# GpSimd's early transfers go ahead of its constants; the scan's first piece goes first; the last tile's outputs share one buffer

## The chip, the cores and the metric

The kernel runs on one core of a Trainium2 chip. Its engines work side by side, each through its own queue of instructions in a fixed order: TensorE (PE; PEld are its weight loads), VectorE (DVE), ScalarE (ACT), GpSimd (POOL) and SyncE (SP, which only issues transfers). Transfers (DMAs) are issued here by GpSimd, SyncE and ScalarE. The metric is the time of one execution on the device in microseconds (us), lower is better.

## What is computed

Causal attention with a selective bias, followed by a layer norm and a two-layer MLP with a residual. There are 8 batches of 8 heads, 576 positions and a head size of 64; the model width is 512 and the hidden width 2048.

```python
# attention, for each batch and head
cum    = np.cumsum(np.maximum(s, 0.0), axis=-1)
scores = q @ k.T / sqrt(64) + np.minimum(-(cum[:, None] - cum[None, :]), 0.0)
attn   = softmax(where(causal, -1e9, scores))
x      = attn @ v                      # heads side by side: (8, 576, 512)
# MLP, for each position
xn  = (x - mean) / sqrt(var + 1e-6) * g_ln
out = x + np.maximum(xn @ w_ch1, 0.0) @ w_ch2
```

## The kernel before, in words

**Scores with the bias inside.** The cumulated sum of s is added to the scores by the matmul itself: k and q get four more rows behind their 64 (68 in all), which hold cum split into three bf16 pieces (hi, mid, lo) and the constants 1 and -1. The tiles `kq[0..2]` hold k and q transposed, with 4 heads each (a group; there are 16). Positions are cut into four tiles of 128 and one of 64.

**Batch 0 is treated apart.** Its k and q come as rows into `rowb`: tile 0 by way of two f32 tiles that SyncE (k) and ScalarE (q) load and ScalarE casts (steps `ck` and `cq`), tiles 1 to 4 by GpSimd transfers that cast on the way (line 148). The bias pieces are added to the rows as columns, and TensorE transposes both (step T), from PSUM to `kq[0]` and `kq[1]` (step e, the evacuation). Groups 2 to 5 come as pairs of heads (line 152, tiles kp and qp, pairs 4 to 11), are transposed by TensorE (step Q, line 276), and get their four extra rows by small SyncE transfers of the pieces (`aug`, lines 212 and 214). The later groups come as rows by SyncE and are transposed by the DMA engines.

**The start.** s is loaded to `c_in`. Three cuts of it (positions 0 to 127, 128 to 255, 256 to 575) go each through relu, scan (the running sum), hi, sub, mid, lo; then TensorE transposes the pieces (step tc) and VectorE puts them into `rowb` (step bc). The steps W are idle matmuls that keep TensorE running.

**Order.** Nothing is scheduled by a tool: the order in which the code issues instructions is the order in every queue. First come the constants and the first transfers; then PLAN, a list of words written out by hand, each a step with its tile, group and engine (`e.0.1:D` is the evacuation of tile 0, group 1 on VectorE); then a loop over the remaining heads n, from head 18 on. The waits between engines come from the tiles that an instruction reads and writes.

**GpSimd's queue.** All transfers that cast come from GpSimd, in one order: the k, q and v tiles of batch 0, the first quarter ("part 0") of the first weight w1, pair 4, tile 4 of batch 0, then w1 part 1, pair 5, w1 part 2, the five v tiles of batch 1, pair 6, w1 part 3, and the second weight and pairs 7 and 8. Between them stand memsets of constants: the pads and constant rows of `kq[2]`, the column of ones in `v_bf[1]` (65th column of each head, which makes the attention's sums), the pad of `er` (the exponentials), constants of `cT`.

**MLP.** `units` of four matmuls each, in a queue of their own that PLAN (words u and U) and the loop draw on, fill TensorE between the attention steps: `mlp1` (line 539) against w1 with a relu to `hT`, `mlp2` (line 557) against the second weight. At its end `mlp2` adds the residual into a buffer `yo` (line 566) and sends it out. The pool `yop` has three such buffers, taken in turn. The last 64 positions of all batches are put together, two batches a tile, and come last (`mixed_units`); the last of these four tiles is cut into three pieces of columns (256, 128, 128), each with a `yo` of its own, and each tile goes out in two transfers, from SyncE and ScalarE (lines 591 and 592).

Of the kernel before, what the change touches and what calls it, by code (L numbers as in the profile page):

```python
# [9 lines left out]
F32 = mybir.dt.float32  # L10
BF16 = mybir.dt.bfloat16
AX = mybir.AxisListType
ALU = mybir.AluOpType
ACT = mybir.ActivationFunctionType

P = 128
# [3 lines left out]
def kernel(  # L20
# [11 lines left out]
    nc = tc.nc  # L32
    B, H, S, D = q.shape
    Dm, Dh = moe_w_ch1.shape
# [4 lines left out]
    NF = S // P  # L39
    NT = NF + 1  # L40
    TL = S - NF * P
    SP = NT * P
    BH = B * H
    KA = D + 4
    OB, OC, OD = 512, 1024, 1536
    EW = 1664
# [5 lines left out]
    KT = 96  # L52
# [10 lines left out]
    yop = ctx.enter_context(tc.tile_pool(name="yop", bufs=3))  # L63
# [8 lines left out]
    ident = const.tile([P, P], BF16, name="ident")  # L72
    maskT = const.tile([P, P], BF16, name="maskT")
# [3 lines left out]
    gb = const.tile([P, Dm], F32, name="gb")  # L77
    rstd = const.tile([P, B, NT], F32, name="rstd")
    mhalf = const.tile([P, 8], F32, name="mhalf")
# [3 lines left out]
    v_bf = [const.tile([P, NT, H, D + 1], BF16, name=f"v_bf{i}") for i in range(2)]  # L83


    kq = [const.tile([P, 2, G, SP], BF16, name=f"kq{i}") for i in range(3)]
# [7 lines left out]
    er = const.tile([P, 4, EW], BF16, name="er")  # L94
# [7 lines left out]
    rowb = const.tile([P, NT, 2 * H, KA], BF16, name="rowb")  # L102
# [26 lines left out]
    def tile_src(kind, t):  # L129
        pn = P if t < NF else TL  # L130
        src = k if kind == "k" else q
        return src[0, :, t * P : t * P + pn, :].rearrange("h s d -> s h d")
# [6 lines left out]
    def ld_tile(kind, t, eng):  # L139
        tmp = stage.tile([P, H, D], F32, name="tiletmp", tag="st")  # L140
        eng.dma_start(out=tmp, in_=tile_src(kind, t))
        loaded[kind, t] = tmp
# [4 lines left out]
    def ld_cast_tile(kind, t):  # L147
        nc.gpsimd.dma_start(out=tile_dst(kind, t), in_=tile_src(kind, t))  # L148

    def ld_cast(kind, g):  # L150
        ready[kind, g] = pair_tile(kind)
        nc.gpsimd.dma_start(out=ready[kind, g][0:QP], in_=pair_src(kind, g))

    def ld_cast_pair(g):
        ld_cast("k", g)
        ld_cast("q", g)

    def ld_cast_v(b, t):
        pn = P if t < NF else TL
        nc.gpsimd.dma_start(  # L160
            out=v_bf[b % 2][:pn, t, :, 0:D],
            in_=v[b, :, t * P : t * P + pn, :].rearrange("h s d -> s h d"),
        )
# [34 lines left out]
    def ld_w1(c):  # L198
        sl = slice(c * 512, (c + 1) * 512)
        nc.gpsimd.dma_start(out=w1_bf[:, :, sl], in_=w1_r[:, :, sl])  # L200
# [348 lines left out]
            nc.scalar.activation(out=hT[:, fb, :], in_=ph, func=ACT.Relu)  # L549

    py = {}

    def mlp2(t, quarter, x, rs, dst, c0=0, c1=512):
        if quarter == 0:
            py[t] = ps_m.tile([P, Dm], F32, name="py", tag="m")[:, 0 : c1 - c0]
        for fb in range(quarter * 4, quarter * 4 + 4):
            nc.tensor.matmul(  # L557
                py[t],
                lhsT=hT[:, fb, t * P : (t + 1) * P],
                rhs=w2_bf[:, fb, c0:c1],  # L560
                start=(fb == 0),
                stop=(fb == FB - 1),
            )
        if quarter == 3:
            yo = yop.tile([P, Dm], F32, name="yo", tag="yo")[:, 0 : c1 - c0]
            nc.vector.scalar_tensor_tensor(  # L566
                out=yo, in0=py[t], scalar=rs, in1=x[:, c0:c1], op0=ALU.mult, op1=ALU.add
            )
            dst(yo, c0, c1)


    def chunk_units(xT_of, of_t, last=False):
        units = [lambda fb=fb: mlp1(xT_of(), fb) for fb in range(FB)]
        for t in range(NF):
            halves = ((0, 256), (256, 384), (384, 512)) if last and t == NF - 1 else ((0, 512),)
            for c in halves:
                for qr in range(4):
                    units.append(lambda t=t, qr=qr, c=c: mlp2(t, qr, *of_t(t), *c))
        return units
# [27 lines left out]
    def keep_warm(n):  # L607
        w = ps_t.tile([P, 512], F32, name="idle", tag="tr")
        for _ in range(n):
            nc.tensor.matmul(w, lhsT=zeros[:, 0:P], rhs=zeros, start=True, stop=True)  # L610
# [7 lines left out]
    )  # L618
    nc.sync.dma_start(out=c_in, in_=s.rearrange("b h s -> (b h) s"))
    ld_tile("k", 0, nc.sync)  # L620

    nc.vector.memset(zeros.bitcast(F32), 0.0)
    nc.vector.memset(warm, 0.0)
# [5 lines left out]
    nc.vector.memset(rowb[:, :, H : 2 * H, D + 1 : KA], 1.0)  # L629
    nc.vector.memset(v_bf[0][:, 0:NF, :, D : D + 1], 1.0)  # L630
    nc.vector.memset(v_bf[0][0:TL, NF, :, D : D + 1], 1.0)
    for i in range(2):
        nc.vector.memset(kq[i][0:KA, 0, :, S:SP], 0.0)
    nc.vector.memset(eight, 1.0 / scale)
    nc.vector.memset(mhalf, -0.5)
    nc.vector.memset(c3[BH:KT], 0.0)
    nc.vector.memset(rowb[TL:KT, NF], 0.0)
    make_identity(nc, ident)
    nc.gpsimd.memset(maskT, 0.0)
    nc.gpsimd.affine_select(  # L640
        out=maskT,
        in_=maskT,
        compare_op=ALU.is_ge,
        fill=-1.0e30,
        base=0,
        pattern=[[1, P]],
        channel_multiplier=-1,
    )
    for t in range(1, NF):
        ld_cast_tile("k", t)  # L650
        ld_cast_tile("q", t)
        ld_cast_v(0, t - 1)
        if t == 1:
            nc.gpsimd.dma_start(out=gb, in_=moe_g_ln.partition_broadcast(P))
    ld_cast_v(0, NF - 1)
    ld_w1(0)
    ld_cast_pair(4)
    ld_cast_tile("k", NF)
    ld_cast_tile("q", NF)
    ld_cast_v(0, NF)  # L660

    nc.gpsimd.memset(kq[2][:, :, :, S:SP], 0.0)
    for u, two in ((0, -1.0058441162109375), (1, 1.0019378662109375)):
        nc.gpsimd.memset(kq[2][D:P, u].bitcast(F32)[:, :, 0 : S // 2], two)  # L664
    ld_w1(1)
    nc.gpsimd.memset(v_bf[1][:, 0:NF, :, D : D + 1], 1.0)
    nc.gpsimd.memset(v_bf[1][0:TL, NF, :, D : D + 1], 1.0)
    for i in range(2):
        nc.gpsimd.memset(v_bf[i][TL:P, NF, :, :], 0.0)
    nc.gpsimd.memset(er[:, :, OD:EW], 0.0)  # L670
    ld_cast_pair(5)
    ld_w1(2)
    nc.gpsimd.memset(cT[:, :, 0, :, 0], -1.0)
    nc.gpsimd.memset(cT[:, :, 1, :, 1:4], 1.0)
    for t in range(NT):
        ld_cast_v(1, t)
    ld_cast_pair(6)
    ld_w1(3)
    ld_w2(0)
    ld_cast_pair(7)  # L680
# [200 lines left out]
    def pv_next():  # L881
# [5 lines left out]
        if ph_ == 7:  # L887
# [6 lines left out]
            out=c_in[:, 0:P], in0=c_in[:, 0:P], scalar=0.0, in1=eight, op0=ALU.max, op1=ALU.mult  # L894
# [18 lines left out]
        "M": piece,  # L913
        "r": piece_relu,
        "W": lambda n: keep_warm(n),
        "Sk": last_scores,
        "xk": last_exp,
        "relur": lambda: nc.scalar.activation(
            out=c_in[:, P:S], in_=c_in[:, P:S], func=ACT.Relu, scale=1.0 / scale
# [20 lines left out]
    }  # L940

    PLAN = """
        relu.0 scan.0 relur hi.0 scan.1 sub.0 hi.1 ck sub.1 mid.0 W.4 mid.1 lo.0 tc.0 bc.0 W.2
        cq T.0.0 scan.2 lo.1 hi.2 e.0.0:D T.0.1 W.2 e.0.1:D sub.2 tc.1 S.0.0.0 x.0.0.0 S.0.1.0
        bc.1 V.0.0 T.1.1 mid.2 N.0.0 x.0.1.0 T.1.0 V.0.1 e.1.1:D S.1.1.0 lo.2 e.1.0:A tc.2 bc.2
        x.1.1.0 S.1.0.0 T.2.0 S.1.1.1 bc.4 T.2.1 e.2.0:D x.1.0.0 S.1.0.1 x.1.1.1 S.2.0.0 T.3.0
        V.1.1 N.0.1 e.2.1:D aug x.2.0.0 x.1.0.1 L.0 S.2.1.0 S.2.0.1 x.2.1.0 S.2.1.1 V.1.0
        e.3.0:D x.2.0.1 T.3.1 N.1.0 N.1.1 S.2.1.2 x.2.1.1 S.2.0.2 x.2.1.2 x.2.0.2 L.1 S.3.0.0
# [112 lines left out]
```

## Time and profile before

| | us |
|---|---|
| median of 3 runs | 353.77 (353.52 to 355.91) |
| the profiled execution | 354.29 |
| its span | 352.6 |
| TensorE busy | 344.4 |
| VectorE busy | 192.2 |
| ScalarE busy | 190.4 |
| GpSimd busy | 162.0 |

The span goes from the first to the last instruction of the program; the execution's own time has 1.7 us around it. In a line of the timeline stand the start in us, the duration, the engine, the line of code, the operation, what is written and read, the shape and the number of instructions taken together, and, in brackets, how long the engine had been idle and what ended that. In the chain of waits stand start, duration and what the chain ran through. A transfer's landing is counted from the start of its issue. GpSimd's rows of transfers are the issuing alone; the data follow later.

In the first 45 us the DMA engines are busy nearly throughout; TensorE has its useful work from 7.65 us on (the first transposes of batch 0) and from 12.2 us on it runs almost without a gap.

### The profile page before, as it was taken

Reading aid. Unit: us, or ns where it says so; the run is one execution under the profiler, and the core shown is the slowest. Engines: PE = TensorE matmul, PEld = TensorE weight load, DVE = VectorE, ACT = ScalarE, POOL = GpSimd, SP = SyncE. Lnnn points to the kernel's source line nnn. Section 1 sums busy time; section 2 is a strip of 40 time slices with the busy share of each in tenths; the row PEclk is TensorE's granted clock in tenths of the full one; section 3 lists DMA queues with packets and bytes.
Section 4 is the critical chain, followed back from the end, with each engine's and each line's share of the span. In section 5 each row is a group of like instructions: output and inputs, shape, how many; then the busy total and the mean of one; then the engine's idle time right before and its main releaser. Section 6 shows DMA issues by size and latency. Waiting matters only on the chain.

```text
span 352.6 us, 8239 instructions
## 1 busy us (share of the span) xinstructions
PE 344.4 (98%) x3110; PEld 196.1 (56%) x3110; DVE 192.2 (55%) x519; ACT 190.4 (54%) x365; POOL 162.0 (46%) x334
## 2 busy tenths in 40 slices
PE   7999999999999999999999999999999999999995
PEld 3898666655555555555555555555555544444444
DVE  7788688964366537562655458443844582113112
ACT  4799798977635673367526662576347403402500
POOL 9996587284455736383756365445521010000000
PEclk9999999999999999999999999999999999999999
DMA  9999999899998999999999999999830033011012
GB/s 150 170 164 150 201 204 129 144 176 143 187 188 132 196 210 178 210 198 176 188 199 205 198 180 171 203 160 200 148 108 0 3 81 112 2 59 59 3 41 79
DMA packets 169160, 50.31 MB, mean 143 GB/s; under 512 B 156896, under 2 KB 164512, under 8 KB 169120
## 3 DMA queue, kind: packets, MB, share of 16 engines
q1 hardware_dynamic: 115168, 36.54, 56.0%
q0 software_dynamic: 52432, 12.46, 41.1%
q10 hardware_dynamic: 1520, 0.79, 0.9%
q8 instruction: 24, 0.39, 0.5%
q14 instruction: 16, 0.13, 0.1%
HBM read 37.11 MB, written 9.44 MB: 132 GB/s over the span
## 4 chain that ended last, share of the span: by engine, by line
PE 81%; DMA 7%; POOL 6%; DVE 2%; issue 1%; SPq 1%; POOLq 0%; DVEq 0%
PE ph L539 32%; PE py L557 32%; PE pot L404 7%; DMA w_bf<-in_moe_w_ch_dram 5%; PE sc L326 3%; PE sb L326 3%; PE sa L326 3%; POOL rowb L148 2%; DMA rowtmp<-in_q_dram 2%; POOL v_bf L160 1%; PE trqk L276 1%; DMA out_dram<-yo 1%; DVE yo L566 1%; SPq L170 1%; POOL kq L664 1%
## 5 line engine op out<-in xcount | busy, mean ns | idle before, releaser
L557 PE MATMUL py<-w_bf,hT 128*128 128x512 bf16 (+2 forms) x608 | 133.6, 368 | 0.0
L539 PE MATMUL ph<-xT,w_bf 128*128 128x512 bf16 x480 | 112.5, 379 | 0.7 <-DMA w_bf<-in_moe_w_ch_dram 0.7
L549 ACT ACTIVATE hT<-ph 128x512 bf16<-128x512 f32 x102 | 60.8, 598 | 73.2 <-PE ph L539 73.2
L557 PEld LDWEIGHTS <-hT 128*128 128x128 bf16 x608 | 54.3, 98 | 52.7
L539 PEld LDWEIGHTS <-w_bf 128*128 128x128 bf16 x544 | 49.5, 98 | 51.3 <-issue 0.8
L337 ACT ACTIVATE er<-sa 128x512 bf16<-128x512 f32 x56 | 33.4, 597 | 59.4 <-PE sa L326 53.0
L346 POOL TENSOR_SCALAR_AFFINE_SELECT er<-er 128x256 bf16<-128x256 bf16 x108 | 44.3, 430 | 35.5 <-ACT er L337 34.7
L547 DVE TENSOR_SCALAR hT<-ph 128x512 bf16<-128x512 f32 x34 | 23.5, 692 | 58.0 <-PE ph L539 50.0
L566 DVE SCALAR_TENSOR_TENSOR yo<-py,rstd,xb 128x512 f32<-128x512 f32 x32 | 23.9, 748 | 35.8 <-PE py L557 34.5
L404 PEld LDWEIGHTS <-er 128*128 128x128 bf16 x840 | 32.9, 98 | 13.1 <-POOL er L346 0.9
L326 PEld LDWEIGHTS <-kq 68*128 68x128 bf16 x400 | 28.5, 97 | 19.8
L160 POOL DMA_DIRECT2D v_bf<-in_v_dram x40 | 34.6, 872 | 2.5 <-PE pot L404 1.8
L404 PE MATMUL pot<-v_bf,er 128*128 128x65 bf16 x840 | 34.9, 194 | 0.4 <-POOL er L346 0.4
L337 ACT ACTIVATE er<-sc 128x512 bf16<-128x512 f32 x56 | 34.1, 610 | 0.0
L337 ACT ACTIVATE er<-sb 128x512 bf16<-128x512 f32 x56 | 33.5, 597 | 0.0
L178 POOL CAST rowb<-rowtmp 128x512 bf16<-128x512 f32 (+1 forms) x25 | 15.3, 610 | 34.4 <-DMA rowtmp<-in_k_dram 14.9
L416 DVE RECIPROCAL rinv<-pot 128x5 f32<-128x5 f32 x56 | 10.8, 192 | 36.9 <-PE pot L404 36.8
L178 POOL CAST kq<-rowtmp 128x512 bf16<-128x512 f32 (+1 forms) x25 | 15.4, 616 | 30.9 <-DMA rowtmp<-in_q_dram 27.5
L418 DVE TENSOR_TENSOR xb<-pot,rinv 128x256 f32<-128x256 f32 x56 | 23.8, 425 | 1.9
L494 DVE SCALAR_TENSOR_TENSOR xn<-xb,mv,gb 128x512 bf16<-128x512 f32 x28 | 22.9, 818 | 1.0
L448 DVE BATCH_NORM_STATS2 stats<-xb 128x6 f32<-128x128 f32 (+1 forms) x84 | 21.9, 320 | 0.3
L326 PE MATMUL sc<-kq 68*128 68x256 bf16 (+1 forms) x192 | 21.7, 228 | 0.0
(118 smaller groups left out, 354.4 us busy)
## 6 DMA issues: line engine op xcount, KB each, us to landing
out_dram<-yo SPq DMA_DIRECT2D x32, 256.0 KB
rowtmp<-in_k_dram SPq DMA_DIRECT2D x40, 128.0 KB
rowtmp<-in_q_dram SPq DMA_DIRECT2D x40, 128.0 KB
v_bf<-in_v_dram POOLq DMA_DIRECT2D x32, 128.0 KB, 5.6
w_bf<-in_moe_w_ch_dram POOLq DMA_DIRECT2D x8, 512.0 KB, 9.7
kp<-in_k_dram POOLq DMA_DIRECT2D x8, 144.0 KB, 7.9
qp<-in_q_dram POOLq DMA_DIRECT2D x8, 144.0 KB, 7.9
rowtmp<-in_k_dram SPq DMA_DIRECT2D x10, 64.0 KB
```

The source lines that it names most:

```text
L160: nc.gpsimd.dma_start(out=v_bf[b % 2][:pn, t, :, 0:D], in_=v[b, :, t * P : t * P + pn, :].rearrange("h s d -> s h d"),)
L178: nc.gpsimd.tensor_copy(out=rows[gam % 2][0:pn, t, :, :, 0:D], in_=loaded.pop(("rows", gam, t))[0:pn])
L326: nc.tensor.matmul(a[:, c + a0 - q0 : c + a1 - q0], lhsT=k_cols(b, h, kb), rhs=cols, start=True, stop=not (pe_mask and diag),)
L337: nc.scalar.activation(out=e[:, o : o + 512], in_=a, func=ACT.Exp, scale=scale)
L346: nc.gpsimd.affine_select(out=two, in_=two, compare_op=ALU.is_ge, fill=0.0, base=0, pattern=[[0, 2], [1, P]], channel_multiplier=-1,)
L404: nc.tensor.matmul(pot[:, t, :], lhsT=e[:, o : o + P], rhs=vv[:, kb, h, :], start=(kb == 0), stop=(kb == last),)
L418: nc.vector.tensor_tensor(out=xb[b][:, :, hs], in0=pot[:, 0:NF, 0:D], in1=rinv[:, 0:NF].unsqueeze(2).to_broadcast([P, NF, D]), op=ALU.mult,)
L539: nc.tensor.matmul(ph, lhsT=w1_bf[:, kd, fb * P : (fb + 1) * P], rhs=xT[:, :, kd, :], start=(kd == 0), stop=(kd == KD - 1),)
L547: nc.vector.tensor_scalar_max(out=hT[:, fb, :], in0=ph, scalar1=0.0)
L549: nc.scalar.activation(out=hT[:, fb, :], in_=ph, func=ACT.Relu)
L557: nc.tensor.matmul(py[t], lhsT=hT[:, fb, t * P : (t + 1) * P], rhs=w2_bf[:, fb, c0:c1], start=(fb == 0), stop=(fb == FB - 1),)
L566: nc.vector.scalar_tensor_tensor(out=yo, in0=py[t], scalar=rs, in1=x[:, c0:c1], op0=ALU.mult, op1=ALU.add)
```

## The change

GpSimd's queue: `ident` and `maskT` are made after the first and second group of three loads, no longer ahead of all. The load of `gb` (the gain of the norm) goes to SyncE. w1 part 1 goes ahead of the memsets of `kq[2]`, and pair 5 ahead of its constant rows. The pads of `kq[0]` and `kq[1]` come to GpSimd from VectorE. The five v tiles of batch 1 go ahead of the pad of `er` and of the ones of `v_bf[1]`, pair 6 ahead of the constants of `cT`.

VectorE's queue: two memsets (`mhalf`, and rows 64 to 95 of the last row tile) go from the start into PLAN, as the step m. In PLAN the first cut's mid and lo go ahead of the second cut's sub, and `cq` goes from behind `bc` to right behind `relur`.

Output: the three pieces of the last tile (and each whole tile) take columns of one `yo`.

```diff
+    yos = {}
...
         if quarter == 3:
-            yo = yop.tile([P, Dm], F32, name="yo", tag="yo")[:, 0 : c1 - c0]
+            if c0 == 0:
+                yos[t] = yop.tile([P, Dm], F32, name="yo", tag="yo")
+            yo = yos[t][:, c0:c1]
...
     ld_tile("k", 0, nc.sync)
+    nc.sync.dma_start(out=gb, in_=moe_g_ln.partition_broadcast(P))
...
-    for i in range(2):
-        nc.vector.memset(kq[i][0:KA, 0, :, S:SP], 0.0)
     nc.vector.memset(eight, 1.0 / scale)
-    nc.vector.memset(mhalf, -0.5)
     nc.vector.memset(c3[BH:KT], 0.0)
-    nc.vector.memset(rowb[TL:KT, NF], 0.0)
-    make_identity(nc, ident)
-    nc.gpsimd.memset(maskT, 0.0)
-    nc.gpsimd.affine_select(
...
     for t in range(1, NF):
         ld_cast_tile("k", t)
         ld_cast_tile("q", t)
         ld_cast_v(0, t - 1)
         if t == 1:
-            nc.gpsimd.dma_start(out=gb, in_=moe_g_ln.partition_broadcast(P))
+            make_identity(nc, ident)
+        if t == 2:
+            nc.gpsimd.memset(maskT, 0.0)
+            nc.gpsimd.affine_select(
...
     ld_cast_v(0, NF - 1)
     ld_w1(0)
     ld_cast_pair(4)
     ld_cast_tile("k", NF)
     ld_cast_tile("q", NF)
     ld_cast_v(0, NF)
-
+    ld_w1(1)
+    for i in range(2):
+        nc.gpsimd.memset(kq[i][0:KA, 0, :, S:SP], 0.0)
     nc.gpsimd.memset(kq[2][:, :, :, S:SP], 0.0)
+    ld_cast_pair(5)
     for u, two in ((0, -1.0058441162109375), (1, 1.0019378662109375)):
         nc.gpsimd.memset(kq[2][D:P, u].bitcast(F32)[:, :, 0 : S // 2], two)
-    ld_w1(1)
+    ld_w1(2)
+    for i in range(2):
+        nc.gpsimd.memset(v_bf[i][TL:P, NF, :, :], 0.0)
+    for t in range(NT):
+        ld_cast_v(1, t)
+    nc.gpsimd.memset(er[:, :, OD:EW], 0.0)
     nc.gpsimd.memset(v_bf[1][:, 0:NF, :, D : D + 1], 1.0)
     nc.gpsimd.memset(v_bf[1][0:TL, NF, :, D : D + 1], 1.0)
-    for i in range(2):
-        nc.gpsimd.memset(v_bf[i][TL:P, NF, :, :], 0.0)
-    nc.gpsimd.memset(er[:, :, OD:EW], 0.0)
-    ld_cast_pair(5)
-    ld_w1(2)
+    ld_cast_pair(6)
     nc.gpsimd.memset(cT[:, :, 0, :, 0], -1.0)
     nc.gpsimd.memset(cT[:, :, 1, :, 1:4], 1.0)
-    for t in range(NT):
-        ld_cast_v(1, t)
-    ld_cast_pair(6)
     ld_w1(3)
     ld_w2(0)
     ld_cast_pair(7)
...
+        "m": lambda: (nc.vector.memset(rowb[TL:KT, NF], 0.0), nc.vector.memset(mhalf, -0.5)),
...
-        relu.0 scan.0 relur hi.0 scan.1 sub.0 hi.1 ck sub.1 mid.0 W.4 mid.1 lo.0 tc.0 bc.0 W.2
-        cq T.0.0 scan.2 lo.1 hi.2 e.0.0:D T.0.1 W.2 e.0.1:D sub.2 tc.1 S.0.0.0 x.0.0.0 S.0.1.0
-        bc.1 V.0.0 T.1.1 mid.2 N.0.0 x.0.1.0 T.1.0 V.0.1 e.1.1:D S.1.1.0 lo.2 e.1.0:A tc.2 bc.2
+        relu.0 scan.0 relur cq hi.0 scan.1 sub.0 hi.1 ck mid.0 lo.0 W.4 sub.1 mid.1 tc.0 bc.0 W.2
+        T.0.0 scan.2 lo.1 hi.2 e.0.0:D T.0.1 W.2 e.0.1:D sub.2 tc.1 S.0.0.0 x.0.0.0 S.0.1.0
+        bc.1 V.0.0 T.1.1 mid.2 N.0.0 x.0.1.0 T.1.0 V.0.1 e.1.1:D S.1.1.0 lo.2 m e.1.0:A tc.2 bc.2
```

More of the change, by code (lines that the diff above doesn't have):

```diff
@@ L631 @@
     nc.vector.memset(v_bf[0][0:TL, NF, :, D : D + 1], 1.0)
-    for i in range(2):
-        nc.vector.memset(kq[i][0:KA, 0, :, S:SP], 0.0)
     nc.vector.memset(eight, 1.0 / scale)
-    nc.vector.memset(mhalf, -0.5)
     nc.vector.memset(c3[BH:KT], 0.0)
-    nc.vector.memset(rowb[TL:KT, NF], 0.0)
-    make_identity(nc, ident)
-    nc.gpsimd.memset(maskT, 0.0)
-    nc.gpsimd.affine_select(
[L641 to L648, printed above, removed]
     for t in range(1, NF):
@@ L653 @@
         if t == 1:
-            nc.gpsimd.dma_start(out=gb, in_=moe_g_ln.partition_broadcast(P))
+            make_identity(nc, ident)
+        if t == 2:
+            nc.gpsimd.memset(maskT, 0.0)
+            nc.gpsimd.affine_select(
+                out=maskT,
+                in_=maskT,
+                compare_op=ALU.is_ge,
+                fill=-1.0e30,
+                base=0,
+                pattern=[[1, P]],
+                channel_multiplier=-1,
+            )
     ld_cast_v(0, NF - 1)
```

## The prediction

> **What bounds the kernel now.** I read the page first, then the chain of waits, the timelines of GpSimd and TensorE for the first 60 us, single transfers' times to landing, and last the timeline of the tail.
>
> ```profile
> PE 344.4 (98%) x3110; PEld 196.1 (56%) x3110; DVE 192.2 (55%) x519; ACT 190.4 (54%) x365; POOL 162.0 (46%) x334
> PE ph L539 <- DMA w_bf<-in_moe_w_ch_dram: 0.7, 1, 0.7
> ```
>
> TensorE is busy for 344.4 of 352.6 us and has one long wait after the start, 0.7 us. Its order is fixed by the plan, so a change can gain only at the two ends and in such waits. It can lose wherever an operand lands after its matmul's turn. The execution took 354.29 us, 1.7 over its span; the runs' median is 353.77, 0.52 less. I sum against 354.29 and take 0.52 off at the end.
>
> The timeline of VectorE at the start, then of GpSimd:
>
> ```profile
> 3.84 0.51 DVE L637 MEMSET rowb<- 32x544 uint32 x1
> 4.38 0.28 DVE L893 SCALAR_TENSOR_TENSOR c_in<-c_in,eight 64x128 f32<-64x128 f32 x1
> ...
> 4.65 0.60 POOL L654 DMA_DIRECT2D gb<-in_moe_g_ln_dram  x1
> 15.31 0.69 POOL L662 MEMSET kq<- 128x512 bf16 x1
> 16.06 2.05 POOL L664 MEMSET kq<- 64x1152 f32 x2
> 18.07 0.77 POOL L200 DMA_DIRECT2D w_bf<-in_moe_w_ch_dram  x1
> 18.88 0.25 POOL L666 MEMSET v_bf<- 128x32 bf16 x1
> 24.32 4.23 POOL L160 DMA_DIRECT2D v_bf<-in_v_dram  x5
> ...
> 31.05 0.79 POOL L200 DMA_DIRECT2D w_bf<-in_moe_w_ch_dram  x1 [1.23 <-DMA w_bf<-in_moe_w_ch_dram]
> 35.47 0.64 POOL L152 DMA_DIRECT2D qp<-in_q_dram  x1 [1.08 <-DMA v_bf<-in_v_dram]
> ```
>
> Two things are to be seen. The s work begins when VectorE's last memset ends, though ACT had c_in at 3.87. And GpSimd waits: w1's part 3 (31.05) for w1's part 2, q of pair 7 (35.47) for the third v tile of batch 1. Both were issued eight transfers earlier: at most eight of GpSimd's are in flight.
>
> **Head.** VectorE loses from its queue two kq memsets (0.31), mhalf (0.07) and rowb (0.51). So relu.0 starts when c_in is there, 3.87 instead of 4.38: 0.5 earlier. mid.0 and lo.0 (0.28 each) no longer stand behind sub.1 (0.28, which waited 0.18 for hi.1 on ACT): 0.4 more. ident, made after three loads, is ready near 4.1 and first needed near 5; maskT near 7.3, needed near 8.4. The two moved memsets of step m (0.58) fit the 0.70 that VectorE idles ahead of 13.19. cq (0.61) moves into the 1.42 that ACT idles ahead of hi.1 (5.86); its tile's packets end at 4.3 in the trace's DMA records, so it costs nothing, and up to 0.3 should the tile come later. What is late next is the k tile: ck now starts at 6.28, right after hi.1, and the T.0.0 transposes follow it. GpSimd's first load starts at 0.81 instead of 1.84, so its packets run beside the k tile's. Bounds: -0.86 (k tile unharmed) to +0.2 (k tile 0.9 late). I take -0.4, the middle, since no row separates them.
>
> In the windows, 42 to 44 us has a DMA share of 1.25 at 200 GB/s, 32 to 34 us 2.90 at 126: more packets at once do not mean more bytes. [...]
>
> **GpSimd's early transfers.** Without the four constants ahead (0.81 to 1.84) the first three loads go 1.03 earlier. gb's issue (0.56) leaves for SyncE, where nothing is queued behind it before 18.14. From the third pair of loads on, everything is 0.56 earlier up to v's last tile, whose issue ends near 14.75. w1 part 1 follows at once (18.07 before), then the two kq pads taken from VectorE (bounds 0.3, VectorE's own time, to 1.5, twice the step of 0.75 of the 128x512 memset; I take 0.75, since together they have fewer elements), kq2's pad 0.75, and k of pair 5 near 17.1. q of pair 5 must wait: with gb gone from the order, the transfer eight before it is w1 part 0, landed at 11.28 + 7.9 = 19.1, now near 18.6. So the two constant fills (2.0) end near 21.2 and w1 part 2 goes at 21.2 (21.98 before). TensorE used all of these with time to spare, so the earlier landings are worth nothing by themselves. The other moved fills are covered too: er's pad (now near 27) is first written over at 34.97, v_bf's tail rows (near 22) are read from 33.5.
>
> The SyncE transfers of c (line 212, 18.14) wait for those fills: they start 3.1 later, near 21.2. Their last packets end at 23.6 in the trace's DMA records, so near 26.7. Scores s.8 read them at 27.99, with the head's gain 27.6. Bounds 0 to 1.3 of wait; I take 0, as the row leaves 0.9. Such a wait would be swallowed by the next one.
>
> **The step that decides.** The ones columns of v_bf[1] (line 666, 0.33 with 667) are now filled after the five loads of that tile, on the queue that issued them. In the trace's records the first v load (3.79) carries a wait on VectorE, whose only earlier work on that tile is its ones columns; the two rowb loads in front carry none. So columns and load of this tile, though disjoint, are ordered against each other. Turned round, the memset waits until the loads have *landed*, and GpSimd's queue stands behind it: pair 6, two cT memsets, w1 part 3, w2 part 0, pairs 7 and 8, w2 part 1, the masks. Call the landing of batch 1's last v tile T. Before:
>
> ```profile
> L160 POOL DMA_DIRECT2D v_bf<-in_v_dram x1: 747/747/747, 27.8 to 27.8; - x1
> DMA to landing us min/median/max: 9.4/9.4/9.4
> ...
> L152 POOL DMA_DIRECT2D qp<-in_q_dram x1: 636/636/636, 35.5 to 35.5; - x1
> DMA to landing us min/median/max: 8.9/8.9/8.9
> ...
> L160 POOL DMA_DIRECT2D v_bf<-in_v_dram x1: 896/896/896, 58.8 to 58.8; - x1
> DMA to landing us min/median/max: 3.7/3.7/3.7
> ```
>
> That is T = 37.2, and q of pair 7 landed at 44.4. After: the stream starts 0.56 earlier, and the thin stretches 24 to 26 us (108 GB/s) and 26 to 28 (149) fill up to the 204 of 22 to 24: 2 x (1 - 108/204) + 2 x (1 - 149/204) = 1.5 us. So T = 37.2 - 0.56 - 1.5 = 35.2; bounds 33 (twice that gain) and 37.2 (none).
>
> From T the queue issues ones 0.33, pair 6 1.25, cT 1.56, w1 part 3 0.78: ended at T + 3.9. The transfer queue has run dry. The load at 58.8, in a nearly idle stretch, took 3.7, of which 0.9 is issue and about 0.8 data: 2.0 to the first bytes. w1 part 3 needs 2.4 of data (w1 part 1 landed at 25.1, v's last tile of batch 0, ahead of it, at 22.8), so it lands at T + 8.3. From there q of pair 7 took 44.4 - 40.4 = 4.0: T + 12.3 = 47.5. TensorE wants it here:
>
> ```profile
> 46.17 0.42 PE L276 MATMUL trqk<-ident,kp 96*128 96x96 bf16 x6
> 46.43 0.25 PE L276 MATMUL trqk<-ident,qp 96*128 96x96 bf16 x2
> ```
>
> It waits about 1.1 us beyond the old course, and whatever the head gained is gone by then. Bounds of this step: T = 33 gives no wait (the head's gain stays), T = 37.2 gives +3.1. Later transfers (w2 parts, pairs 9 to 11) have over 2 us in hand, and masks of s.10 come near 43.5 for a use at 46.85.
>
> [...]
>
> **Tail.** The chain ends so:
>
> ```profile
> 345.55 2.64 DMA out_dram<-yo
> ...
> 348.64 0.05 DVEq L566
> ...
> 348.73 0.35 DVE yo L566
> ```
>
> The last 128 columns wait for the buffer that tile 2's output still leaves; TensorE was done at 348.26. With one buffer for the three pieces the wait goes: -0.4. Bounds: -0.44 to 0.
>
> **Sum.** 354.29 + 1.1 - 0.4 = 355.0 in the profile; less 0.52, **354.5** in runs.
>
> **Rivals.**
> - *The wait does not bite* (0.25): memset and loads are not ordered, or T is below 34. Then head and tail stay, -0.4 to -1.3, and perhaps the 0.7 wait at 39.43 goes: 351.8 to 353.0. For it: the columns are truly disjoint. Against: the first v load's wait.
> - *Evacuations wait for the kq pads* (0.05), slower: the pads stand ahead of the plan, now on GpSimd until about 16.3. Should the first evacuation (8.45) be ordered behind them as v's load is behind its ones, TensorE starts 8 late: near 361. It decides if the pads' end is ahead of that copy. Against: the rowb loads, in columns beside memset columns, carry no wait.
> - *One buffer puts the pieces in a row* (0.05), slower: each write of yo waits for the output before it, 2.1 to 2.6 each: two waits less what they cover, +3.4 at the end, near 358. Against: the three transfers of c, which read parts of one tile, wait each for its own part.
>
> **How the numbers follow.** The forecast has 0.65: 353.4 to 356.5, from T alone. Range 352.5 to 357.0: it cuts the lower half of the first rival and the two slow ones. A measurement here tells 1% (3.5 us). Faster by more would need half of TensorE's whole idle time: 0.01. Slower by more: the two slow rivals and a tail of T, 0.13. Within: 0.86.
>
> **What would show it.** GpSimd idle before line 666's memset, ended by a v transfer, near 28 to 35 us; TensorE waiting for kp or qp near 46; relu.0 near 3.9; no wait ahead of the last yo. Wrong if GpSimd runs through from the v loads to pair 6.

## The result, and the profile after

The changed kernel takes **356.8 us** (median of 12 executions, 354.48 to 359.55) against 353.99 (12 executions, 353.04 to 355.91) of the kernel before: 1.0077 times as long, with a 95% interval of 1.0051 to 1.0103. The profiled execution took 356.71, span 354.9 (before: 354.29 and 352.6). The forecast was 354.5, the range 352.5 to 357.0: the time lies 0.2 below the range's upper end.

The page of the changed kernel: busy time of each engine, then TensorE's waits (us in total, how often, the longest).

```profile
PE 345.2 (97%) x3086; PEld 197.8 (56%) x3110; DVE 193.4 (55%) x517; ACT 190.9 (54%) x365; POOL 162.9 (46%) x335
...
PE sa L326 <- POOL er L673: 1.4, 1, 1.4
...
PE ph L539 <- DMA xT<-xn: 0.7, 1, 0.7
PE trqk L276 <- DMA kp<-in_k_dram: 0.4, 1, 0.4
PE trqk L276 <- DMA qp<-in_q_dram: 0.3, 1, 0.3
```

Before, the longest wait after the start was one of 0.7, at 39.43; it is gone. Now there are waits in three places: at s.8 (line 326; 1.45 us to two decimals), at the transposes of pair 7 (line 276) and, at 116 us, at line 539 for xT. GpSimd's timeline:

```profile
1.33 1.06 POOL L148 DMA_DIRECT2D rowb<-in_k_dram  x1 [0.81 <-POOLq L1047]
...
19.57 0.63 POOL L152 DMA_DIRECT2D qp<-in_q_dram  x1 [1.48 <-DMA w_bf<-in_moe_w_ch_dram]
20.24 2.05 POOL L667 MEMSET kq<- 64x1152 f32 x2
...
35.19 0.25 POOL L674 MEMSET v_bf<- 128x32 bf16 x1 [6.45 <-DMA v_bf<-in_v_dram]
...
38.53 0.81 POOL L200 DMA_DIRECT2D w_bf<-in_moe_w_ch_dram  x1
39.32 0.78 POOL L203 DMA_DIRECT2D w_bf<-in_moe_w_ch_dram  x1
40.05 0.68 POOL L152 DMA_DIRECT2D kp<-in_k_dram  x1
40.69 0.68 POOL L152 DMA_DIRECT2D qp<-in_q_dram  x1
```

The fourth of these lines is the step that decides: GpSimd stands for 6.45 us until the last v tile lands, at 35.19. The chain of waits runs straight through it to TensorE:

```profile
26.58 8.48 DMA v_bf<-in_v_dram
...
35.19 0.25 POOL v_bf L674
...
40.69 8.28 DMA qp<-in_q_dram
...
49.01 0.43 PE trqk L276 x6
```

The same transpose ran at 46.43 before: 2.58 later, and from there to 116 us every instruction of TensorE stays that much later.

Follow the lag (the start of an instruction after, less that of the same one before) and the loss has more parts than the forecast had. It is -0.30 from the first scores to 27 us; +1.16 after s.8; +2.39 at 37 us; +1.50 at 43 (the old kernel's wait at 39.43 is not there now); +2.59 from 49 us; +2.86 from 117; the tail takes back 0.44. The step between 29 and 37 us stands in the windows. Columns: the stretch, its length, busy time (and instructions) of PE, PEld, DVE, ACT and POOL, the granted TensorE clock, DMA share, GB/s.

```profile
28.00:29.00 1.00, 0.00 (x0) 0.00 (x0) 0.96 (x3) 0.33 (x1) 0.70 (x2) 1.00 2.26 158
29.00:30.00 1.00, 0.85 (x9) 0.63 (x10) 0.90 (x2) 0.32 (x1) 0.00 (x0) 1.00 2.43 167
30.00:31.00 1.00, 1.00 (x22) 0.99 (x20) 0.00 (x0) 1.00 (x3) 0.00 (x0) 0.66 2.35 146
31.00:32.00 1.00, 1.00 (x20) 1.00 (x18) 0.00 (x0) 0.97 (x2) 0.00 (x0) 0.50 1.62 55
32.00:33.00 1.00, 1.00 (x12) 1.00 (x10) 0.42 (x1) 0.98 (x3) 0.00 (x0) 0.50 0.49 19
33.00:34.00 1.00, 1.00 (x15) 1.00 (x14) 0.00 (x0) 0.88 (x3) 0.00 (x0) 0.63 0.27 35
34.00:35.00 1.00, 1.00 (x21) 1.00 (x19) 0.79 (x1) 0.55 (x1) 0.00 (x0) 1.00 0.11 11
```

TensorE stands still for 1.45 us before s.8, runs 1.2 us at full clock, and then at half clock until 33.7. In the last column the transfer queue runs dry, as foreseen: from 31 us on 55 GB/s, then 19, 35 and 11, while GpSimd waits.

### The profile page after: what moved, and what is told of

Its sections match the earlier page's. It is cut to its first block, busy times and chain, and to the rows that moved or that the text cites. A ratio compares the mean times of both kernels' runs of the same rounds, so it can differ in the third digit from the quotient of the medians.

```text
span 354.9 us, 8211 instructions
## 1 busy us (share of the span) xinstructions
PE 345.2 (97%) x3086; PEld 197.8 (56%) x3110; DVE 193.4 (55%) x517; ACT 190.9 (54%) x365; POOL 162.9 (46%) x335
## 4 chain that ended last, share of the span: by engine, by line
PE 81%; DMA 9%; POOL 6%; DVE 2%; issue 2%; POOLq 0%
PE py L558 32%; PE ph L539 32%; PE pot L404 7%; PE sc L326 3%; PE sb L326 3%; PE sa L326 3%; DMA v_bf<-in_v_dram 2%; DMA qp<-in_q_dram 2%; DMA w_bf<-in_moe_w_ch_dram 2%; POOL v_bf L160 2%; DMA xT<-xn 2%; POOL rowb L148 1%; PE trqk L276 1%; POOL kq L667 1%; DVE xb L418 0%
## 5 line engine op out<-in xcount | busy, mean ns | idle before, releaser
L558 PE MATMUL py<-w_bf,hT 128*128 128x512 bf16 (+2 forms) x584 | 130.9, 367 | 1.3
L346 POOL TENSOR_SCALAR_AFFINE_SELECT er<-er 128x256 bf16<-128x256 bf16 x108 | 45.8, 446 | 32.7 <-ACT er L337 32.0
L326 PEld LDWEIGHTS <-kq 68*128 68x128 bf16 x400 | 28.5, 97 | 21.2 <-POOL er L673 1.5
L494 DVE SCALAR_TENSOR_TENSOR xn<-xb,mv,gb 128x512 bf16<-128x512 f32 x28 | 23.9, 853 | 1.0
L326 PE MATMUL sa<-kq 68*128 68x512 bf16 x56 | 21.3, 381 | 1.4 <-POOL er L673 1.4
```

What stands on the lines that cost most here:

```text
L326: nc.tensor.matmul(a[:, c + a0 - q0 : c + a1 - q0], lhsT=k_cols(b, h, kb), rhs=cols, start=True, stop=not (pe_mask and diag),)
L346: nc.gpsimd.affine_select(out=two, in_=two, compare_op=ALU.is_ge, fill=0.0, base=0, pattern=[[0, 2], [1, P]], channel_multiplier=-1,)
L494: nc.vector.scalar_tensor_tensor(out=xn, in0=tiles[t], scalar=mvs[b][:, t, 0:1] if b > 0 else mean0[:, t : t + 1], in1=gb, op0=ALU.subtrac ...
L558: nc.tensor.matmul(py[t], lhsT=hT[:, fb, t * P : (t + 1) * P], rhs=w2_bf[:, fb, c0:c1], start=(fb == 0), stop=(fb == FB - 1),)
```

## The experiments

The theories. **Q**: the ones memset waits for the landing of the v tiles, q of pair 7 is late, and earlier lags are swallowed by that. **S** (in the first expectations): the price is the extra load on the transfers or on GpSimd by itself, wherever the memset stands. **P** (in the second): the prices of the waits add up. **H**: gb's load on SyncE's queue delays GpSimd's first loads. **K**: TensorE's half clock comes from a stand-still. Each experiment ran beside the kernel before, which took 353.8 to 354.2 there.

| kernel | us | ratio to before (95%) |
|---|---|---|
| changed | 356.8 (354.48 to 359.55) | 1.0077 (1.0051 to 1.0103) |
| ones first | 354.53 (353.4 to 357.16) | 1.0004 (0.998 to 1.0028) |
| fills first | 357.19 (356.28 to 360.21) | 1.0086 (1.0051 to 1.0121) |
| both | 353.34 (352.64 to 355.22) | 0.998 (0.9957 to 1.0003) |
| ones first, TensorE kept busy | 355.13 (354.51 to 356.41) | 1.0028 (1.0006 to 1.005) |
| 66 columns | 355.27 (353.39 to 357.48) | 1.0045 (1.0021 to 1.0069) |
| both, gb back | 353.15 (352.53 to 357.06) | 0.999 (0.9966 to 1.0015) |
| before + gb on SyncE | 354.55 (353.59 to 356.42) | 1.0031 (1.0012 to 1.0051) |
| changed, TensorE kept busy | 356.01 (354.72 to 359.47) | 1.0068 (1.0037 to 1.01) |
| before + ones late | 358.16 (357.23 to 361.1) | 1.0116 (1.007 to 1.0162) |
| changed, gb back | 357.02 (355.39 to 358.26) | 1.0085 (1.006 to 1.011) |
| before + tail | 353.66 (352.95 to 355.12) | 0.999 (0.9965 to 1.0014) |

In the row "changed, gb back" one execution of 732 us, which no trace shows, is left out of the span in brackets.

### Which wait costs: ones first, fills first, both

```diff
+    nc.gpsimd.memset(v_bf[1][:, 0:NF, :, D : D + 1], 1.0)       # ones first
+    nc.gpsimd.memset(v_bf[1][0:TL, NF, :, D : D + 1], 1.0)
     for t in range(NT):
         ld_cast_v(1, t)
...
+    for u, two in ((0, -1.0058441162109375), (1, 1.0019378662109375)):   # fills first
+        nc.gpsimd.memset(kq[2][D:P, u].bitcast(F32)[:, :, 0 : S // 2], two)
     ld_cast_pair(5)
```

> The changed kernel with the ones of v_bf[1] filled ahead of the five v loads of batch 1, as before the change; all else of the change stays. Theory Q (the memset behind the loads empties the transfer queue): GpSimd's 6.45 us of idle near 29 to 35 us and TensorE's waits for kp and qp near 48 us are gone; the wait at s.8 (1.5 us) and the slow clock behind it stay, so TensorE is about 1.5 behind the kernel before until the end, less 0.4 in the tail: 355.0 to 355.9. Rival S (the price is the extra load on the transfers or on GpSimd by itself, wherever the memset stands): no difference from the changed kernel, 356.4 to 357.2.

> The changed kernel with the two constant fills of kq[2] ahead of pair 5, so that they no longer stand behind q of pair 5, which waits for w1 part 0. The SyncE transfers of c start near 19 instead of 22.3 and the 1.5 us wait at s.8 and the slow clock behind it go. Theory Q: the waits for kp and qp of pair 7 swallow that gain, since their landing near 49 us stays: 356.4 to 357.2, as the changed kernel. Rival P (the prices add up): 2.4 less than the changed kernel, 354.2 to 354.6.

> Both of these edits in the changed kernel. Theory Q: neither wait is left; what stays is the head (0.3 earlier) and the tail (0.4), perhaps without the 0.9 wait at 39.4 of the kernel before: 352.3 to 353.5, faster than the kernel before by 0.1 to 0.5%. Rival: the early transfers cost something elsewhere, and it is no faster than before: 354 or more.

With the ones ahead of the loads 2.3 us of the 2.8 are gone, more than expected (355.0 to 355.9): in this profile TensorE had already stood 1.05 us for v in the head, so its wait at s.8 was 0.6, and no half clock followed. GpSimd runs through (no idle but the 0.27 in brackets):

```profile
25.61 0.24 POOL L671 MEMSET v_bf<- 128x32 bf16 x1
25.67 0.21 POOL L672 MEMSET v_bf<- 64x8 bf16 x1
26.15 4.21 POOL L160 DMA_DIRECT2D v_bf<-in_v_dram  x5 [0.27 <-POOL v_bf L672]
30.31 0.58 POOL L675 MEMSET er<- 128x512 bf16 x1
30.78 0.69 POOL L152 DMA_DIRECT2D kp<-in_k_dram  x1
```

The four kernels form a square. Moving the constant fills forward, which lets the transfers of c start before 21.4 and removes the wait at s.8, is worth 1.2 us when the ones are early (354.53 to 353.34) and nothing when they are late (356.8 to 357.19): the wait for q of pair 7 swallows it. Q stands; S, with 356.4 to 357.2 for "ones first", and P, with 354.2 to 354.6 for "fills first", fall. In the profile with both, TensorE waits neither at s.8 nor for kp or qp. (The profile of "fills first" can't show the gain at s.8: after 2.0 us of waiting in the head, TensorE came there only at 31.8.) Even without its two waits the change can't be told from the kernel before: the interval of "both" reaches from 0.9957 to 1.0003.

### What orders memset and loads: 66 columns

```diff
-    v_bf = [const.tile([P, NT, H, D + 1], BF16, ...
+    v_bf = [const.tile([P, NT, H, D + 2], BF16, ...
```

> The changed kernel with 66 columns of v_bf per head instead of 65 (the 66th is never written or read; it computes the same). The order of GpSimd's instructions is untouched: the ones columns of v_bf[1] still stand behind its five loads. Theory Q (memset and loads are ordered because a row of 65 two-byte numbers lets a load's last bytes and the ones column share a four-byte word; with 66 they don't, so the memset runs through): no idle of GpSimd ahead of the ones memset, q of pair 7 issued near 35 to 36, no wait of TensorE for kp or qp near 47, and the time of the kernel with the memsets ahead of the loads: 354.0 to 355.2. Rival (the order hangs on the tile as a whole): the idle of 6.45 us stays, 356.3 to 357.3.

The GpSimd timeline of this kernel:

```profile
28.82 0.53 POOL L673 MEMSET er<- 128x512 bf16 x1
29.28 0.26 POOL L674 MEMSET v_bf<- 128x32 bf16 x1
29.34 0.21 POOL L675 MEMSET v_bf<- 64x8 bf16 x1
29.39 0.65 POOL L152 DMA_DIRECT2D kp<-in_k_dram  x1
```

The memset stands where the change put it, behind the five loads, and waits for nothing, though the last v tile lands at 33.8; TensorE has no wait for kp or qp. So the order between memset and load is not owed to the tile as a whole. It goes with rows of 65 two-byte numbers (GpSimd idle for 6.45 us ahead of the memset) and is gone with 66 (no idle there). That a shared four-byte word is the reason was argued, not shown. The time, 355.27, is 1.5 below the changed kernel's and just above the range expected (354.0 to 355.2); the wait at s.8 is still in it, this time named by what it waits for:

```profile
PE pot L777 <- DMA v_bf<-in_v_dram: 1.2, 1, 1.2
PE sa L326 <- DMA kq<-c: 0.9, 1, 0.9
```

In the changed kernel's page that wait is put down to the memset of er, which ended at 28.75, a tenth of a microsecond ahead of the landing of c's last transfer (28.84, TensorE's release 28.87). The kernel "both", whose memset of er runs nearly as late (27.81 to 28.4) but whose c transfers go 2.2 earlier, has no such wait: there line 326 ran at 28.09, before that memset had ended. So s.8 waited for c. Its transfers, before and in the changed kernel:

```profile
18.14 0.76 SPq L212 DMA_DIRECT2D kq<-c  x1
```

```profile
22.32 0.77 SPq L212 DMA_DIRECT2D kq<-c  x1
```

### The price alone: before + ones late

```diff
-    nc.gpsimd.memset(v_bf[1][:, 0:NF, :, D : D + 1], 1.0)
-    nc.gpsimd.memset(v_bf[1][0:TL, NF, :, D : D + 1], 1.0)
...
     for t in range(NT):
         ld_cast_v(1, t)
+    nc.gpsimd.memset(v_bf[1][:, 0:NF, :, D : D + 1], 1.0)
+    nc.gpsimd.memset(v_bf[1][0:TL, NF, :, D : D + 1], 1.0)
```

> The kernel before with one edit: the two ones memsets of v_bf[1] behind its five v loads instead of ahead of kq's tail rows. Theory Q (the memset waits for the last v landing T, the transfer queue runs dry, q of pair 7 is late): GpSimd idle ahead of the memset until T, 36 to 37.2 by the old profile. Here the two cT memsets (1.5) stand ahead of the loads, so by the prediction's prices q of pair 7 lands at T + 10.8, by those of the changed kernel's profile (T + 13.8 with the cT memsets) at T + 12.3: 47.5 to 49.5, against TensorE's turn at 46.43. So 1.1 to 3.1 more than before: 355.0 to 357.0. Rival (the loss of the changed kernel comes from its other edits, and this wait is swallowed by them): 353.6 to 354.3.

Two moved memsets of 0.3 us cost 4.4 us, more than the whole change and more than expected. T was 36.0, the early end of what was expected, and q of pair 7 landed at 49.82, T + 13.8, not T + 12.3: w1's part 3 took 7.8 us from issue to landing. Pair 6, too, was late here, and that had not been priced: TensorE stood 1.8 us for its q and then ran at half clock.

```profile
39.00:40.00 1.00, 0.49 (x3) 0.00 (x0) 0.57 (x2) 0.73 (x2) 1.00 (x3) 1.00 1.06 153
40.00:41.00 1.00, 0.00 (x0) 0.00 (x0) 0.00 (x0) 0.12 (x1) 1.00 (x3) 1.00 0.61 88
...
43.00:44.00 1.00, 1.00 (x5) 0.43 (x4) 0.99 (x3) 0.97 (x3) 0.86 (x2) 0.50 0.97 142
44.00:45.00 1.00, 1.00 (x4) 0.36 (x3) 0.36 (x1) 0.94 (x2) 0.00 (x0) 0.50 1.07 162
45.00:46.00 1.00, 1.00 (x3) 0.29 (x2) 0.95 (x3) 0.00 (x0) 0.45 (x1) 0.50 1.12 172
```

### gb's new queue: before + gb on SyncE; both, gb back; changed, gb back

```diff
-            nc.gpsimd.dma_start(out=gb, in_=moe_g_ln.partition_broadcast(P))
...
     ld_tile("k", 0, nc.sync)
+    nc.sync.dma_start(out=gb, in_=moe_g_ln.partition_broadcast(P))
```

gb is 256 KB, not the 512 that the second expectation names.

> The kernel before with one edit: gb's load goes to SyncE, behind the k tile, and leaves GpSimd's order. Theory H: the first v tile lands 0.5 to 2.7 us later than 8.87, TensorE waits for it near 10 to 11; half of this is made good by waits that come later, so 354.3 to 355.3. Rival B (same bytes): GpSimd's later transfers go 0.56 earlier, nothing is late: 353.5 to 354.2.

> The changed kernel with ones memsets ahead of the v loads and the constant fills of kq[2] ahead of pair 5 (that one took 353.3), and gb's load back on GpSimd's queue behind the first v load. Theory H (gb's 512 KB on SyncE's queue share the DMA engines with GpSimd's first loads from 5.5 to 8 us, so that v's first tile lands at 10.0 to 11.6 instead of 8.9 and TensorE waits for it near 10, differently in every execution): the first v tile lands by 9.4, no wait of TensorE for v_bf near 10, TensorE ahead of the old kernel by 0.3 at 24 us where the profiles of the earlier experiments have 0.1 to 3.8 behind; 352.6 to 353.2, and a smaller spread than 2.6 us. Rival B (the same bytes move either way, and gb's issue costs GpSimd 0.6): 353.2 to 353.9, same spread.

> The changed kernel with one edit: gb's load back on GpSimd's queue behind the first v load. Theory H + Q (gb on SyncE delays the first loads and makes the head uneven; the wait for q of pair 7 then swallows a lead or a lag of the head, but not a lag over 3 us): first v tile by 9.4, no wait of TensorE for v_bf near 10, GpSimd still idle ahead of the ones memset, q of pair 7 still late by 2.5 to 3.5; median 356.0 to 357.0, hardly below the changed kernel's 356.8, but its executions of 358 and 359 are gone. Rival (gb's move costs in the median as it does alone, 0.7): 355.6 to 356.1.

The first v tile's load, in the kernel before and with gb alone moved; it was issued at 3.79 in both, so it landed at 8.9 and at 11.2:

```profile
L160 POOL DMA_DIRECT2D v_bf<-in_v_dram x1: 893/893/893, 3.8 to 3.8; - x1
DMA to landing us min/median/max: 5.1/5.1/5.1
```

```profile
L160 POOL DMA_DIRECT2D v_bf<-in_v_dram x1: 896/896/896, 3.8 to 3.8; - x1
DMA to landing us min/median/max: 7.4/7.4/7.4
```

By the trace's records the first v tile lands at 8.8 to 9.6 in all five profiles with gb on GpSimd's queue and at 10.0 to 11.6 in all eight with gb on SyncE's: on its own queue gb no longer stands behind the three loads that TensorE needs first, it goes beside them (in the changed kernel issued at 2.07 and landed at 8.16, ahead of that tile's 9.96; before, issued at 4.65 and landed at 9.60, behind its 8.87). TensorE then waits for v near 10 us, 0.8 to 2.0 in seven of the eight profiles (in "before + gb on SyncE" the view names ScalarE's er for it, but the tile landed at 11.22 and TensorE went on at 11.36) and not at all in the changed kernel's own. Alone the move costs 0.7 in the median: H holds. With gb back the lead of the head is there, 0.36 and 0.59. But it is not kept: in "both, gb back" it is gone at 25.4 us, in a stand-still of 0.47 ahead of T.4.1 for which the view names no releaser, and the 0.2 gained on "both" can't be told from nothing. Nor is the spread smaller, as had been expected: one execution took 357.06 (the other eleven lie between 352.53 and 353.64). In "changed, gb back" it only makes the stand-still at s.8 longer (1.8 us instead of 1.5), and the median stays, as expected; the executions at 358.1 and 358.3 stay too, and only those above are gone.

### TensorE's clock: kept busy through the stand-still

```diff
-        ... x.4.1.1 s.8 ...
+        ... x.4.1.1 W.7 s.8 ...
```

> The first of these kernels (ones ahead of the loads) with seven idle matmuls of 512 columns (1.5 us) put right in front of s.8, where TensorE waits 1.5 us. They add work that nobody needs. Theory K (the granted clock falls to a half because TensorE stood still): the clock stays at 1.00 from 30 to 34 us, and the kernel is about 0.9 faster than the first one, 354.1 to 355.0. Rival: the slow stretch comes from something else, such as the transfers; then it stays and the time is that of the first one or up to 0.3 more.

> The changed kernel with seven idle matmuls (0.21 us each) ahead of s.8, where TensorE stood still for 1.5 us. Theory K (a stand-still of 1.5 us or more is what halves TensorE's clock afterwards; of the changed kernel's 12 executions six have a mean clock of 0.995, median 357.6, and six 0.998 to 1.0, median 356.3): no stretch of half clock between 28 and 36 us, hardly an execution at 0.995, q of pair 7 swallows what is won: 355.9 to 356.6. Rival (the halving is not tied to the stand-still): clocks and time as in the changed kernel, 356.6 to 357.2.

The first of these missed: without filler the profile of "ones first" has a stand-still of 0.6 at s.8 and no half clock there, so nothing was to be won, and the median is 0.6 worse. The second came out as K foresaw, but doesn't settle it: eight of ten executions have a mean clock of 0.998 or more (six of twelve without filler), and the median is 0.8 lower, but neither difference is clear of noise (the ratios to the kernel before, 1.0068 and 1.0077, have intervals that overlap). Its profile has a clock of 1.00 from 24 to 40 us, but can't test K there: TensorE came to s.8 at 31.5, when c had landed (30.5), and would not have waited. It has a half-clock stretch elsewhere, after the head's 2.0 us of waiting for v:

```profile
10.00:11.00 1.00, 0.00 (x0) 0.00 (x0) 0.00 (x0) 0.55 (x2) 1.00 (x2) 1.00 2.43 155
11.00:12.00 1.00, 0.37 (x9) 0.40 (x10) 0.04 (x1) 0.00 (x0) 0.91 (x2) 1.00 2.42 154
12.00:13.00 1.00, 1.00 (x19) 1.00 (x17) 0.96 (x4) 0.00 (x0) 0.96 (x2) 0.74 2.41 154
13.00:14.00 1.00, 0.96 (x13) 0.85 (x11) 0.83 (x3) 0.96 (x1) 0.68 (x2) 0.50 2.43 155
...
18.00:19.00 1.00, 1.00 (x13) 1.00 (x11) 0.91 (x3) 0.00 (x0) 1.00 (x4) 0.50 1.49 187
19.00:20.00 1.00, 1.00 (x21) 1.00 (x20) 0.86 (x2) 0.77 (x2) 0.61 (x2) 0.84 1.96 173
```

### The tail alone

```diff
+            if c0 == 0:
+                yos[t] = yop.tile([P, Dm], F32, name="yo", tag="yo")
+            yo = yos[t][:, c0:c1]
```

> The kernel before with the tail edit alone (last tile's pieces share one yo buffer). The prediction's step: the last write of yo (348.73 in the old profile) no longer waits for the buffer of tile 2's output, 0.44 earlier: 353.3 to 353.7 beside 353.9 of the kernel before. Rival (the pieces wait for each other's outputs): 356 to 358.

The last write of yo waits 0.54, for its matmuls, where it waited 0.98 for a buffer. The first line is of the kernel before, the second of this one:

```profile
348.73 0.35 DVE L566 SCALAR_TENSOR_TENSOR yo<-py,rstd,xm 128x128 f32<-128x128 f32 x1 [0.98 <-PE py L557]
```

```profile
347.99 0.35 DVE L569 SCALAR_TENSOR_TENSOR yo<-py,rstd,xm 128x128 f32<-128x128 f32 x1 [0.54 <-PE py L558]
```

That is the 0.44 of the prediction. The medians, 353.66 and 353.79, differ by less than they can tell. The rest of this profile's difference comes from elsewhere: the wait of 0.7 at 39.43 in the old profile was 0.2 here, in a part of the program that this edit doesn't touch.

## Why the prediction was right, and where it was not

**The step that decides: right in cause and place.** The memset behind the loads waited for the last v tile; T, foreseen at 35.2, was 35.19; the queue ran dry; TensorE waited for pair 7. Undoing that order alone takes 2.3 of the 2.8 us away, widening the rows by one column 1.5.

**That T came out so well was luck.** It was to come 0.56 earlier, and 1.5 from thin stretches filling up to 204 GB/s. The first of the five loads went 0.36 earlier (23.96, before 24.32), and the two stretches, 24 to 26 and 26 to 28 us, had 171 and 170 GB/s; put into the same sum, these give 36.0. What ended last was not the stream of bytes: of the sixteen counts of the last v tile's semaphore, fifteen were in by 33.51, and the last came at 35.21, while 11 to 35 GB/s moved. Why that one came so late stays open.

**Mis-sized: what follows T.** The prediction drew its narrower band, 353.4 to 356.5, from T alone. T was hit, and the time still lies above that band, inside the range only by what was added to it; the error is in the term after T. The sum had q of pair 7 at T + 12.3; it landed at 48.97, T + 13.8. Of the 1.5 between, the issues up to w1 part 3 took 4.15 instead of 3.9; part 3 landed 5.27 after that issue ended, not 4.4 (of which the 2.4 for the data are 2.25 by the two rows named, 25.04 less 22.79); and pair 7 came 4.36 behind it, not 4.0. The restart was slower than "2.0 to the first bytes, then 204 GB/s": 23 GB/s from 39 to 40 us and 42 from 40 to 41, then 197 and 211, but 170 and 179 from 43 to 45. The 2.0 was an estimate: of the 3.7 us of the load at 58.8 the issue's 0.9 stands in a row, the 0.8 for its data in none. This term alone makes +2.6 where the forecast had +1.1. From issue to landing the 512 KB of part 3 took 6.1 us here and 7.8 in "before + ones late".

**Also wrong: the profile's distance to the median.** 0.52 was taken off because the old profile lay above its median of three. The new profile lies 0.1 below its median, so that distance didn't carry over. Of the 2.3 us between 354.5 and 356.8, 1.5 belong to the term above, 0.6 to this, and the rest to the new wait of 0.72 at 116 us for xT, less one of 0.37 at 120 us that is gone. (A smaller slip: at T = 33 the head's gain was to stay, which makes 353.0, not 353.4, the lower end of the narrower band.)

**GpSimd's queue before T: the mechanism right, a microsecond off.** q of pair 5 waited for w1 part 0 as worked out (eight in flight), at 19.57 instead of 18.6. The first load was issued at 1.33, not 0.81, for GpSimd's sequencer held it up (the 0.81 in brackets), and ident and maskT, now between the loads, took 1.3 there, more than the earlier start (0.51) and gb's leaving (0.56) had saved. So the fills ended at 22.3 (21.2 foreseen), the transfers of c went at 22.32, and s.8 waited 1.5, just beyond the bound of 1.3. Taking 0 was wrong, by a reading too: 23.6 is the end of c's last packets, but the transfers' last semaphore count came at 24.41 (in the changed kernel 28.21 and 28.84), which left 0.1 and not 0.9; that such a wait "would be swallowed by the next one" was right, as the square of four shows.

**The head: right in size, not in what limits it.** The lead was 0.30 (0.4 foreseen), and relu.0 ran at 3.98 (3.87 foreseen). But the k tile was not late: its last count came at 6.18 (6.25 before), its cast ended at 6.82, and the transposes T.0.0 ran at 7.29. They stood behind bc.0, which waited 0.50 for tc.0 on TensorE; lo.0 had ended at 6.24, and tc.0 came at 6.62, behind the kernel's own idle matmuls. The first 13 of these took 5.51 us, before 4.47: each took 0.43 until 6.4, before until 4.2 and then 0.21. Why they went at the slow pace for longer stays open; in other profiles of the same instructions T.0.0 ran at 6.84 to 7.29. What was missed as well is gb: "nothing is queued behind it" looked at issues and not at bytes. The prediction weighed a late k tile; it was GpSimd's own first loads that paid (9.96 for the first v tile, issued 0.53 earlier than before, against 8.87).

**The tail:** 0.44, as worked out. **The early transfers:** worth nothing, as said; w1 part 1 went 2.4 us earlier and landed at 25.04 in both profiles.

**The rivals.** That the wait doesn't bite was refuted; its price, 351.8 to 353.0, was too low, for the kernels without the waits take 353.15 and 353.34. The evacuations waited for no pads: the first scores ran at 8.88 (9.18 before). The shared yo put nothing in a row.

## What to carry to other kernels

A memset that moves behind a load of the same tile may wait for the load's landing, and everything queued behind it on that engine, transfers above all, waits too (6.45 us here): ask the trace which loads already carry a wait on a fill of their tile. Here rows of 66 two-byte elements instead of 65 took the wait away; one pair of kernels shows it, and not why. A transfer that leaves one queue for another still moves its bytes: with gb on SyncE's queue the loads that had been ahead of it on GpSimd's landed later (first v tile at 10.0 to 11.6 us, not 8.8 to 9.6). The waits in this chain didn't add up: several lags lay before the same late transfer, and taking away an earlier one (at s.8, or gb's) was worth nothing until that was gone (357.19 and 357.02, where the changed kernel takes 356.8).

## What was not expected of the hardware

**After a stand-still of 1.5 us or more TensorE ran at half clock.** The longest stand-still of each profile after the first useful matmuls, and the half clock that began 0.4 to 1.5 us after its end (its length from the clock of the windows: 0.66 in a stretch of 1 us is 0.68 us at half). The three profiles not in the table have none over 0.8 us and no half clock.

| kernel | stand-still, us | half clock, us |
|---|---|---|
| both; before + gb on SyncE; ones first; ones first, busy; 66 columns | 0.8; 0.9; 1.0; 1.1; 1.2 | none |
| changed | 1.5 | 3.4 |
| changed, gb back; before + ones late | 1.8; 1.8 | 3.4; 3.4 |
| fills first; changed, busy | 2.0; 2.0 | 6.8; 6.8 |

The half clock lasted 3.4 us or twice that. A stand-still of 1.5 us was enough in these profiles and one of 1.2 was not. That the stand-still is the cause is argued from this table; no kernel took one away and nothing else. Where between 1.2 and 1.5 us the bound lies, and why 2.0 us brought 6.8 us at half clock and 1.8 us brought 3.4, stays open. The executions of the changed kernel differ in the same way: the six with a mean clock of 0.995 have a median of 357.6, the six at 0.998 to 1.0 one of 356.3; where the half clock lay in those that were not traced isn't known.

**The landing of the first loads varies between executions** with gb on SyncE's queue: 10.0 to 11.6 for the first v tile over the seven profiles that share the changed kernel's first 15 us. Why it varies stays open. So does why the wait at 39.43 of the old profile is 0.2 to 0.7 in some profiles of unchanged code there and absent in others.
